# Batch 0's spectral stage: full-width forward matmuls on a three-part table, one product per pair of frequencies, and inverse tables loaded once and copied by Pool

## The chip, the cores and the metric

The kernel runs on one core of a Trainium2 chip. The core has a matrix engine (TensorE, PE in the profile, with its weight loads as PEld), a vector engine (VectorE, DVE), a scalar engine (ScalarE, ACT), a general engine (GpSimd, POOL) and a synchronisation engine (SyncE, SP) that here only issues transfers. Each engine works through its own queue in order and waits on semaphores. Sixteen DMA engines move data; a transfer is issued from Pool's queue (software descriptors; it may convert float32 to float16 and add on the way) or from SP's. The metric is the device time of one execution in microseconds; lower is better.

## The reference

For each of 8 batches, x (3008 x 256) is filtered along its 3008 positions in the frequency domain, and then a two-layer network with a PReLU is applied to every row:

```python
X = np.fft.rfft(x, axis=1)
F = (filt_r + 1j * filt_i)[None, :, :]
y = np.fft.irfft(X * F, n=x.shape[1], axis=1)
...
h = x @ w_in                                    # x is y as 24064 rows of 256; w_in 256 x 2048
g = np.maximum(h, 0.0) + alpha * np.minimum(h, 0.0)
return (g @ w_out).astype(np.float32)           # w_out 2048 x 256
```

Inputs and output are float32; the kernel computes in float16 with float32 sums in PSUM.

## The kernel before

**The transform.** 3008 = 47 x 64. A transform of 47 (piece_a), a twiddled transform of 64 for each of 24 frequencies k1 (piece_b), the product with the filter, the inverse of 64 (piece_c) and the inverse of 47 (piece_d) make the filter; between them the data is turned so that the next sum runs over partitions. The tables are constants in HBM: twf (forward) and twi (inverse), 128 partitions x 24 frequencies x 128 columns each, the left 64 columns and the right 64 holding the real and the imaginary outputs. filt_s holds the filter, filt_r on partitions 0 to 63 and filt_i on 64 to 127 at first. Frequencies are handled in twelve pairs kp, with k1 = 2 kp and 2 kp + 1.

**Batch 0 (class First)** comes alone at the start, with nothing else to do for the engines, and its turns are made on TensorE with an identity (turn_at, L273; piece_t, L310) instead of through DRAM. Its piece_b (L281) forms for a pair the real outputs twice (both halves of px) and the imaginary ones twice (both halves of pz), by eight matmuls with 64 table columns each (L288), into one PSUM tile of two banks (hps, two buffers). VectorE multiplies px and pz by the filter into uu and ww (L292, L293). piece_c (L296) multiplies uu with twi and ww with twx (L305, L306), where twx is twi with its partition halves exchanged and one negated; it adds up in PSUM (op, two buffers, psO) and ScalarE evicts it into v (L245). twx lies in the last three of the 17 buffers gtb, which the network needs later; its first quarter is formed by VectorE from twi (cross, L353), the rest is loaded.

**The order around it** is written out by hand. Pool issues, in this order: x of batch 0, four quarters of twf, filter and twi (the third load of each table takes two quarters) with twx, then w_in (win_s), w_out (wout_s), x of batch 1, and a copy of half of the filter to filts_s (L378). Each load from Pool waits until the eighth load before it has landed. SP issues five small constants and nothing else until batch 1's first save (L182). TensorE runs piece_a of batch 0 with some idle matmuls (warm), then in turn piece_c(kp), turn_at(kp + 3) and piece_b(kp + 2) (L372), then piece_t and piece_d, and then the network.

**The network and the other batches.** Rows go through in blocks of up to 512; a block takes 16 steps, each with two up matmuls (L421) of this block and the down matmuls (L440) of the block before. After every second step ScalarE evicts 1024 columns into gtb (L427) and VectorE applies the PReLU (L430, L431). A plan puts the transform's pieces of the later batches on numbered steps (put), where they are issued ahead of the step's matmuls. These batches use class Fft: piece_b multiplies px once with filt_s and once with filts_s (L200, L201), and a DMA adds one product's halves crosswise to the other (L203). For that filt_s must hold the real filter on both halves and filts_s the imaginary one, negated on one half: the four operations neg (L481) on steps 17, 20, 23 and 26 and a copy by DMA on step 29 (L485) see to it. Batch 1 starts with piece_a on steps 16 to 31, piece_b from step 40 on.

Of the kernel before, what the change touches and what calls it, by code (L numbers as in the profile page):

```python
# [10 lines left out]
FP16 = mybir.dt.float16  # L11
# [5 lines left out]
NK1 = 24  # L17
D = 256
# [18 lines left out]
def _build_consts():  # L37
# [27 lines left out]
    twf[:64, :, :64], twf[64:, :, :64] = c, s  # L65
    twf[:64, :, 64:], twf[64:, :, 64:] = -s * g, c * g
# [9 lines left out]
def kernel(  # L76
# [16 lines left out]
    twx_np = np.concatenate([twi_np[64:], -twi_np[:64]])  # L93
    twx_d = nc.inline_tensor(twx_np.astype(np.float16), name="c_twx")
# [21 lines left out]
    twf_s = konst.tile([128, NK1, 128], FP16, name="twf_s")  # L116
# [44 lines left out]
    class Fft:  # L161
# [31 lines left out]
        def piece_b(self, kp):  # L193
            px = bank().rearrange("p (k d) -> p k d", k=2)
            for kh in range(2):
                k1 = 2 * kp + kh
                nc.tensor.matmul(px[:, kh], twf_s[:, k1], self.at[:, k1], start=True, stop=True)  # L197
# [55 lines left out]
    class First(Fft):  # L253
# [27 lines left out]
        def piece_b(self, kp):  # L281
            hp = psH.tile([128, 2, 512], FP32, name="hps")
            px, pz = (hp[:, i].rearrange("p (k d) -> p k d", k=2) for i in range(2))
            for i, ps in enumerate((px, pz)):
                for kh in range(2):
                    k1 = 2 * kp + kh
                    for o in (0, 64):
                        nc.tensor.matmul(ps[o : o + 64, kh], twf_s[:, k1, 64 * i : 64 * i + 64],  # L288
                                         self.at[:, k1], start=True, stop=True)
            uu = p_uw.tile([128, 2, D], FP16, name="uu", bufs=4)  # L290
            ww = p_uw.tile([128, 2, D], FP16, name="ww")
            nc.vector.tensor_mul(uu, px, filt_s[:, 2 * kp : 2 * kp + 2])  # L292
            nc.vector.tensor_mul(ww, pz, filt_s[:, 2 * kp : 2 * kp + 2])  # L293
            self.uw[kp] = uu, ww
# [33 lines left out]
    for g in range(4):  # L328
        ka, kb = 6 * g, 6 * g + 6
        kc = slice(ka, 24 if g == 2 else kb)  # L330
        if g < 3:
            nc.gpsimd.dma_start(out=twf_s[:, kc], in_=twf_d.ap()[:, kc])
        load_filt(filt_s, 0, filt_r, ka, kb)
        load_filt(filt_s, 64, filt_i, ka, kb)
        if g < 3:
            nc.gpsimd.dma_start(out=twi_s[:, kc], in_=twi_d.ap()[:, kc])
        if g > 0:
            nc.gpsimd.dma_start(out=twx_s[:, ka:kb], in_=twx_d.ap()[:, ka:kb])
    for kt in range(2):
        nc.gpsimd.dma_start(out=win_s[:, kt], in_=moe_w_in[kt * 128 : (kt + 1) * 128])  # L340
    for q in range(2):
# [5 lines left out]

    def warm(n):
        pw = psO.tile([128, 2, D], FP32, name="op")
        for _ in range(n):  # L350
            nc.tensor.matmul(pw[:, 0, 0:128], id16, id16, start=True, stop=True)

    def cross(ka, kb):  # L353
        nc.vector.tensor_copy(twx_s[0:64, ka:kb], twi_s[64:128, ka:kb])
        nc.vector.tensor_scalar(twx_s[64:128, ka:kb], twi_s[0:64, ka:kb], -1.0, None, OP.mult)

    warm(36)
    for i in range(16):
        f0.piece_a(i, both[i % 2], i % 2 == 1)
        if i % 4 == 3:  # L360
            warm((16, 6, 5, 8)[i // 4])
    alp = psO.tile([128, 2, D], FP32, name="op")
    nc.tensor.transpose(alp[:, 0, 0:16], al16, id32)
    nc.vector.tensor_copy(al_s, alp[:, 0, 0:16])
    nc.vector.tensor_scalar(alm_s, al_s, 1.0, -1.0, OP.mult, OP.add)
    f0.turn_at(0, on_act)
    f0.turn_at(1, on_dve)
    f0.piece_b(0)
    cross(0, 6)
    f0.turn_at(2, on_act)  # L370
    f0.piece_b(1)
    for kp in range(12):  # L372
        f0.piece_c(kp, on_act)
        if kp < 9:
            f0.turn_at(kp + 3, on_act)
# [178 lines left out]
```

## Time and profile before

| | |
|---|---|
| time, median of 3 runs | 797.27 us (796.84 to 797.43) |
| the profiled execution, its own time | 795.65 us |
| its span, first to last instruction | 793.9 us |
| granted TensorE clock | 0.999 |
| busy over the span: PE, PEld | 775.0 us (98%), 538.5 us (68%) |
| DVE, ACT, POOL | 621.2 us (78%), 596.9 us (75%), 193.2 us (24%) |
| DMA moved | 100.58 MB, 127 GB/s on average |

The page is of one profiled execution. Busy time is when an engine had an instruction; the windows give it for stretches of the span, and the chain of waits goes back from one instruction to what released it, and so on. A row of the timeline gives start, duration, engine, line, operation, what is written and read with its shape (partitions x elements), and in brackets the idle time before it with its releaser. The landing of a transfer is when its last part has arrived.

### The profile page before, as it was taken

How to read it: one execution, taken by the hardware profiler on the slowest of the kernel's cores; microseconds unless marked ns; L12 is line 12 of the kernel's file. 1: busy time of each engine (PE TensorE's matmuls, PEld its weight loads, DVE VectorE, ACT ScalarE, POOL GpSimd, SP SyncE). 2: the span in 40 equal slices, each digit the busy share in tenths (PEclk: the TensorE clock that was granted, in tenths of full speed). 3: DMA queues.
4: the chain of work that ended last, by engine and by line, in shares of the span. 5: the costliest groups of instructions: out<-in, count | busy, mean ns of one | idle time of the engine just before them, and what ended most of it. 6: DMA issues, size and time to landing. Idle time of an engine off the chain costs nothing.

```text
span 793.9 us, 16103 instructions
## 1 busy us (share of the span) xinstructions
PE 775.0 (98%) x5956; PEld 538.5 (68%) x5956; DVE 621.2 (78%) x1377; ACT 596.9 (75%) x836; POOL 193.2 (24%) x269
## 2 busy tenths in 40 slices
PE   7999999999999999999999999999999999999997
PEld 6756656666677666766667666766667766766665
DVE  4797985788788787888787877887878888777773
ACT  3788678878778887788768887688867777787663
POOL 7510441153123221341223311242212222000000
PEclk9999999999999999999999999999999999999999
DMA  9967557695776648574684657656494333511111
GB/s 187 209 142 194 115 112 175 192 180 118 150 173 113 138 102 192 123 147 101 149 189 82 135 120 167 152 109 139 101 212 90 66 77 81 138 36 28 41 40 54
DMA packets 102310, 100.58 MB, mean 127 GB/s; under 512 B 11320, under 2 KB 92744, under 8 KB 102104
## 3 DMA queue, kind: packets, MB, share of 16 engines
q1 hardware_dynamic: 79512, 68.80, 32.9%
q0 software_dynamic: 22720, 30.75, 24.3%
q8 instruction: 47, 0.77, 0.4%
q14 instruction: 31, 0.25, 0.1%
HBM read 56.26 MB, written 46.66 MB: 130 GB/s over the span
## 4 chain that ended last, share of the span: by engine, by line
PE 89%; ACT 4%; DMA 3%; DVE 2%; issue 1%; SPq 0%; POOL 0%; ACTq 0%; DVEq 0%; POOLq 0%
PE hps L421 38%; PE op L440 38%; PE psF L177 3%; PE psF L238 3%; ACT gtb L427 2%; PE psF L216 2%; PE psF L197 2%; DMA uu<-ww 1%; DMA filt_s<-in_filt_i_dram 1%; DMA xs<-in_x_dram 1%; ACT asb L245 1%; PE hps L288 1%; PE psF L317 1%; DMA v_dram<-v 0%; DMA zt<-v_dram 0%
## 5 line engine op out<-in xcount | busy, mean ns | idle before, releaser
L427 ACT ACTIVATE gtb<-hps 128x1024 f16<-128x1024 f32 (+1 forms) x384 | 385.4, 1005 | 133.3 <-PE hps L421 127.9
L440 PE MATMUL op<-wout_s,gtb 128*128 128x256 f16 x3008 | 451.1, 272 | 0.6 <-DVE gtb L431 0.6
L421 PE MATMUL hps<-yT,win_s 128*128 128x512 f16 (+1 forms) x1536 | 449.2, 374 | 0.4 <-ACT gtb L427 0.2
L440 PEld LDWEIGHTS <-gtb 128*128 128x128 f16 x3008 | 293.2, 98 | 189.6 <-DVE gtb L431 0.9
L430 DVE TENSOR_SCALAR m<-gtb,alm_s 128x512 f16<-128x512 f16 (+1 forms) x768 | 235.7, 349 | 126.7 <-ACT gtb L427 124.4
L431 DVE TENSOR_TENSOR gtb<-gtb,m 128x1024 f16<-128x1024 f16 (+1 forms) x384 | 261.6, 681 | 19.9
L203 POOL DMA_DIRECT2D uu<-ww x168 | 140.6, 980 | 438.3 <-PE hps L421 322.1
L421 PEld LDWEIGHTS <-win_s 128*128 128x128 f16 x1536 | 145.3, 98 | 30.9 <-issue 3.1
L245 ACT ACTIVATE asb<-psF 96x512 f16<-96x512 f32 x112 | 66.2, 591 | 11.5 <-PE psF L177 11.4
L245 ACT ACTIVATE yT<-psF 128x376 f16<-128x376 f32 x120 | 57.1, 485 | 13.3 <-PE psF L238 12.8
L445 ACT ACTIVATE osb<-op 128x512 f32<-128x512 f32 x96 | 56.1, 585 | 6.1 <-issue 3.2
L245 ACT ACTIVATE v<-psF 128x512 f16<-128x512 f32 x84 | 49.4, 595 | 10.8 <-PE psF L216 10.0
L200 DVE TENSOR_TENSOR ww<-psF,filts_s 128x512 f16<-128x512 f32 x84 | 57.4, 684 | 0.0
L201 DVE TENSOR_TENSOR uu<-psF,filt_s 128x512 f16<-128x512 f32 x84 | 57.2, 681 | 0.0
L139 POOL DMA_DIRECT2D xs<-in_x_dram x64 | 43.9, 946 | 25.8 <-PE psF L177 15.0
L177 PE MATMUL psF<-xs,wf_s 94*96 94x512 f16 x112 | 42.7, 381 | 1.5 <-ACT v L245 1.0
L238 PE MATMUL psF<-wi_s,zt 96*128 96x94 f16 x504 | 40.3, 205 | 1.9 <-DMA zt<-v_dram 1.0
L238 PEld LDWEIGHTS <-zt 96*128 96x128 f16 x512 | 34.3, 97 | 6.2 <-issue 1.5
L216 PE MATMUL psF<-uu,twi_s 128*128 128x256 f16 x168 | 31.3, 273 | 2.3 <-ACT yT L245 0.9
L197 PE MATMUL psF<-at,twf_s 128*128 128x256 f16 x168 | 32.1, 273 | 0.3 <-ACT asb L245 0.2
L216 PEld LDWEIGHTS <-twi_s 128*128 128x128 f16 x168 | 15.7, 98 | 5.9 <-DMA uu<-ww 2.7
L197 PEld LDWEIGHTS <-twf_s 128*128 128x128 f16 x168 | 15.8, 98 | 2.8 <-DVE uu L201 0.7
(55 smaller groups left out, 173.3 us busy)
## 6 DMA issues: line engine op xcount, KB each, us to landing
out_dram<-osb SPq DMA_DIRECT2D x128, 128.0 KB
xs<-in_x_dram POOLq DMA_DIRECT2D x64, 188.0 KB, 5.4
a_dram<-asb SPq DMA_DIRECT2D x28, 384.0 KB
uu<-ww POOLq DMA_DIRECT2D x168, 64.0 KB, 2.9
v_dram<-v SPq DMA_DIRECT2D x112, 96.0 KB
zt<-v_dram SPq DMA_DIRECT2D x28, 384.0 KB
at<-a_dram SPq DMA_DIRECT2D x20, 384.0 KB
at<-a_dram SPq DMA_DIRECT2D x32, 96.0 KB
```

Of the source, the lines that this page charges most:

```text
L177: nc.tensor.matmul(ps[0:96], wf1_s, xs[:, o : o + 512], start=True, stop=True)
L197: nc.tensor.matmul(px[:, kh], twf_s[:, k1], self.at[:, k1], start=True, stop=True)
L200: nc.vector.tensor_mul(ww, px, filts_s[:, 2 * kp : 2 * kp + 2])
L203: nc.gpsimd.dma_start(out=uu[o : o + 64], in_=ww[64 - o : 128 - o], accum_op=OP.add)
L216: nc.tensor.matmul(pv[:, kh], twi_s[:, k1], u[:, kh], start=u is us[0], stop=u is us[-1])
L238: nc.tensor.matmul(ps[:, m], self.zt[:, 8 * g + 4 * mh + m, dh * 128 : dh * 128 + 128], wi3_s, start=True, stop=True)
L245: nc.scalar.activation(o, i, AF.Copy)
L421: nc.tensor.matmul(self.hps[:, j % 2, 0:tn], win_s[:, kt, j * 128 : (j + 1) * 128], yT[:, kt, self.t0 : self.t0 + tn], start=(kt == 0), st ...
L427: nc.scalar.activation(g[:, :, 0:tn], self.hps[:, :, 0:tn], AF.Copy)
L430: nc.vector.tensor_scalar(m[:, i, 0:tn], g[:, i, 0:tn], 0.0, a, OP.min, OP.mult)
L431: nc.vector.tensor_add(g[:, :, 0:tn], g[:, :, 0:tn], m[:, :, 0:tn])
L440: nc.tensor.matmul(self.op[:, si % 2], self.gts[k][:, 128 * si : 128 * si + 128], wout_s[:, k], start=(k == 0), stop=(k == 15))
```

## The change

- The forward table becomes three parts wide in SBUF: 64 columns with the imaginary outputs, 64 with the real ones, and a third part that is the first negated, formed on chip by third() from the loaded first part (ScalarE for frequencies 0 to 11, VectorE for 12 to 23). piece_b of batch 0 multiplies with columns 64 to 191 and with 0 to 127: four matmuls of 128 columns for a pair instead of eight of 64. The other batches use columns 64 to 191.
- VectorE multiplies both results of a pair by the filter in one operation, on 1024 columns of PSUM with the filter read twice, and writes into eight of the buffers gtb.
- twx is no longer a table of its own. SP loads partitions 0 to 63 of twi into the same partitions of twi_s, and 64 to 127 into those of twx_s (load_twi), in three parts, each after two one-element copies on VectorE or ScalarE that fix when it may start; Pool copies each half to the other partitions (both_halves). So in batch 0 both halves of each table are equal, and the signs stand in the forward table. Before the later batches a DMA copies partitions 64 to 127 of twx_s to twi_s, which then holds twi as before.
- The loads are re-ordered: twf still in quarters, the filter in parts of 4, 6, 7 and 7 frequencies, Pool's copies among them, w_in after six copies and w_out after all ten. The table twf is now loaded into the first 128 of 192 columns.
- The order of the pieces in batch 0: piece_b(kp + 2), turn_at(kp + 4), piece_c(kp - 2), with c7 to c11 in the last three turns, c10 evicted by VectorE.
- The filter for the later batches: filts_s is now two copies by DMA of the imaginary half, and neg writes the negated real half into filt_s, on steps 26, 29, 32 and 35. The copy on step 29 is gone.

```diff
--- before.py
+++ after.py
@@ -62,8 +62,8 @@
     ang = 2 * np.pi * s2[:, None, None] * kk[None, :, :] / NFFT
     c, s = np.cos(ang), np.sin(ang)
     twf = np.empty((128, NK1, 128))
-    twf[:64, :, :64], twf[64:, :, :64] = c, s
-    twf[:64, :, 64:], twf[64:, :, 64:] = -s * g, c * g
+    twf[:64, :, 64:], twf[64:, :, 64:] = c, s
+    twf[:64, :, :64], twf[64:, :, :64] = -s * g, c * g
     ec, es = c.transpose(2, 1, 0), s.transpose(2, 1, 0)
     gp = g[:, None, None]
     twi = np.empty((128, NK1, 128))
@@ -90,8 +90,6 @@
     wi3_d = nc.inline_tensor(wi3_np.astype(np.float16), name="c_wi3")
     twf_d = nc.inline_tensor(twf_np.astype(np.float16), name="c_twf")
     twi_d = nc.inline_tensor(twi_np.astype(np.float16), name="c_twi")
-    twx_np = np.concatenate([twi_np[64:], -twi_np[:64]])
-    twx_d = nc.inline_tensor(twx_np.astype(np.float16), name="c_twx")
     id_d = nc.inline_tensor(np.eye(128, dtype=np.float16), name="c_id")
     wfx_np = wf1_np.reshape(2 * N1, 2, 2, NK1).transpose(0, 3, 2, 1).reshape(2 * N1, 96)
     wfx_d = nc.inline_tensor(np.ascontiguousarray(wfx_np).astype(np.float16), name="c_wfx")
@@ -113,7 +111,7 @@
 
     wf1_s = konst.tile([2 * N1, 96], FP16, name="wf1_s")
     wi3_s = konst.tile([96, 2 * N1], FP16, name="wi3_s")
-    twf_s = konst.tile([128, NK1, 128], FP16, name="twf_s")
+    twf_s = konst.tile([128, NK1, 192], FP16, name="twf_s")
     twi_s = konst.tile([128, NK1, 128], FP16, name="twi_s")
     filt_s = konst.tile([128, NK1, D], FP16, name="filt_s")
     filts_s = konst.tile([128, NK1, D], FP16, name="filts_s")
@@ -194,7 +192,7 @@
             px = bank().rearrange("p (k d) -> p k d", k=2)
             for kh in range(2):
                 k1 = 2 * kp + kh
-                nc.tensor.matmul(px[:, kh], twf_s[:, k1], self.at[:, k1], start=True, stop=True)
+                nc.tensor.matmul(px[:, kh], twf_s[:, k1, 64:192], self.at[:, k1], start=True, stop=True)
             uu = p_uw.tile([128, 2, D], FP16, name="uu", bufs=4)
             ww = p_uw.tile([128, 2, D], FP16, name="ww")
             nc.vector.tensor_mul(ww, px, filts_s[:, 2 * kp : 2 * kp + 2])
@@ -280,18 +278,15 @@
 
         def piece_b(self, kp):
             hp = psH.tile([128, 2, 512], FP32, name="hps")
-            px, pz = (hp[:, i].rearrange("p (k d) -> p k d", k=2) for i in range(2))
-            for i, ps in enumerate((px, pz)):
+            for i in range(2):
                 for kh in range(2):
                     k1 = 2 * kp + kh
-                    for o in (0, 64):
-                        nc.tensor.matmul(ps[o : o + 64, kh], twf_s[:, k1, 64 * i : 64 * i + 64],
-                                         self.at[:, k1], start=True, stop=True)
-            uu = p_uw.tile([128, 2, D], FP16, name="uu", bufs=4)
-            ww = p_uw.tile([128, 2, D], FP16, name="ww")
-            nc.vector.tensor_mul(uu, px, filt_s[:, 2 * kp : 2 * kp + 2])
-            nc.vector.tensor_mul(ww, pz, filt_s[:, 2 * kp : 2 * kp + 2])
-            self.uw[kp] = uu, ww
+                    nc.tensor.matmul(hp[:, i, D * kh : D * kh + D], twf_s[:, k1, 64 - 64 * i : 192 - 64 * i],
+                                     self.at[:, k1], start=True, stop=True)
+            uw = gtb[:, 6 + kp % 8]
+            f = filt_s[:, 2 * kp : 2 * kp + 2].rearrange("p k d -> p (k d)").unsqueeze(1).to_broadcast([128, 2, 512])
+            nc.vector.tensor_mul(uw, hp, f)
+            self.uw[kp] = tuple(uw[:, i].rearrange("p (k d) -> p k d", k=2) for i in range(2))
 
         def piece_c(self, kp, evict):
             uu, ww = self.uw.pop(kp)
@@ -325,57 +320,93 @@
     nc.sync.dma_start(out=wf1_s, in_=wf1_d.ap())
     nc.sync.dma_start(out=wi3_s, in_=wi3_d.ap())
     make_identity(nc, id32)
-    for g in range(4):
-        ka, kb = 6 * g, 6 * g + 6
-        kc = slice(ka, 24 if g == 2 else kb)
-        if g < 3:
-            nc.gpsimd.dma_start(out=twf_s[:, kc], in_=twf_d.ap()[:, kc])
+
+    def third(eng, ka, kb):
+        o, i = twf_s[:, ka:kb, 128:192], twf_s[:, ka:kb, 0:64]
+        if eng is nc.scalar:
+            nc.scalar.activation(o, i, AF.Copy, scale=-1.0)
+        else:
+            nc.vector.tensor_scalar(o, i, -1.0, None, OP.mult)
+
+    def load_twf(ka, kb):
+        nc.gpsimd.dma_start(out=twf_s[:, ka:kb, 0:128], in_=twf_d.ap()[:, ka:kb])
+
+    def load_twi(ka, kb, ev):
+        ev(twi_s[0:1, ka, 0:1], id16[0:1, 0:1])
+        ev(twx_s[64:65, ka, 0:1], id16[64:65, 0:1])
+        nc.sync.dma_start(out=twi_s[0:64, ka:kb], in_=twi_d.ap()[0:64, ka:kb])
+        nc.sync.dma_start(out=twx_s[64:128, ka:kb], in_=twi_d.ap()[64:128, ka:kb])
+
+    def both_halves(ka, kb):
+        nc.gpsimd.tensor_copy(twi_s[64:128, ka:kb], twi_s[0:64, ka:kb])
+        nc.gpsimd.tensor_copy(twx_s[0:64, ka:kb], twx_s[64:128, ka:kb])
+
+    def load_g(ka, kb):
         load_filt(filt_s, 0, filt_r, ka, kb)
         load_filt(filt_s, 64, filt_i, ka, kb)
-        if g < 3:
-            nc.gpsimd.dma_start(out=twi_s[:, kc], in_=twi_d.ap()[:, kc])
-        if g > 0:
-            nc.gpsimd.dma_start(out=twx_s[:, ka:kb], in_=twx_d.ap()[:, ka:kb])
+
+    load_twf(0, 6)
+    load_g(0, 4)
+    load_twf(6, 12)
+    load_g(4, 10)
+    load_twf(12, 18)
+    load_g(10, 17)
+
+    def warm(n):
+        pw = psO.tile([128, 2, D], FP32, name="op")
+        for _ in range(n):
+            nc.tensor.matmul(pw[:, 0, 0:128], id16, id16, start=True, stop=True)
+
+    warm(36)
+    for i in range(16):
+        f0.piece_a(i, both[i % 2], i % 2 == 1)
+        if i % 4 == 3:
+            warm((16, 6, 5, 8)[i // 4])
+        if i == 7:
+            load_twi(0, 4, on_dve)
+        if i == 14:
+            load_twi(4, 12, on_act)
+    alp = psO.tile([128, 2, D], FP32, name="op")
+    nc.tensor.transpose(alp[:, 0, 0:16], al16, id32)
+    third(nc.scalar, 0, 6)
+    f0.turn_at(0, on_act)
+    f0.turn_at(1, on_dve)
+    nc.vector.tensor_copy(al_s, alp[:, 0, 0:16])
+    nc.vector.tensor_scalar(alm_s, al_s, 1.0, -1.0, OP.mult, OP.add)
+    f0.piece_b(0)
+    f0.turn_at(2, on_act)
+    f0.piece_b(1)
+    both_halves(0, 4)
+    load_twf(18, 24)
+    load_g(17, 24)
+    both_halves(4, 8)
+    both_halves(8, 12)
     for kt in range(2):
         nc.gpsimd.dma_start(out=win_s[:, kt], in_=moe_w_in[kt * 128 : (kt + 1) * 128])
+    third(nc.scalar, 6, 12)
+    f0.turn_at(3, on_act)
+    for kp in range(12):
+        if kp < 10:
+            if kp in (3, 6):
+                third(nc.vector, 2 * kp + 6, 2 * kp + 12)
+            f0.piece_b(kp + 2)
+        if kp < 8:
+            f0.turn_at(kp + 4, on_act)
+        if kp == 0:
+            load_twi(12, 24, on_act)
+            both_halves(12, 18)
+            both_halves(18, 24)
+        for k in {9: (7, 8), 10: (9, 10), 11: (11,)}.get(kp, (kp - 2,) if kp > 1 else ()):
+            f0.piece_c(k, on_dve if k == 10 else on_act)
     for q in range(2):
         nc.gpsimd.dma_start(
             out=wout_s[:, 8 * q : 8 * q + 8],
             in_=moe_w_out[1024 * q : 1024 * q + 1024].rearrange("(j p) d -> p j d", p=128))
     for c in range(4):
         xc[(1, c)] = load_x(1, c)
-
-    def warm(n):
-        pw = psO.tile([128, 2, D], FP32, name="op")
-        for _ in range(n):
-            nc.tensor.matmul(pw[:, 0, 0:128], id16, id16, start=True, stop=True)
-
-    def cross(ka, kb):
-        nc.vector.tensor_copy(twx_s[0:64, ka:kb], twi_s[64:128, ka:kb])
-        nc.vector.tensor_scalar(twx_s[64:128, ka:kb], twi_s[0:64, ka:kb], -1.0, None, OP.mult)
-
-    warm(36)
-    for i in range(16):
-        f0.piece_a(i, both[i % 2], i % 2 == 1)
-        if i % 4 == 3:
-            warm((16, 6, 5, 8)[i // 4])
-    alp = psO.tile([128, 2, D], FP32, name="op")
-    nc.tensor.transpose(alp[:, 0, 0:16], al16, id32)
-    nc.vector.tensor_copy(al_s, alp[:, 0, 0:16])
-    nc.vector.tensor_scalar(alm_s, al_s, 1.0, -1.0, OP.mult, OP.add)
-    f0.turn_at(0, on_act)
-    f0.turn_at(1, on_dve)
-    f0.piece_b(0)
-    cross(0, 6)
-    f0.turn_at(2, on_act)
-    f0.piece_b(1)
-    for kp in range(12):
-        f0.piece_c(kp, on_act)
-        if kp < 9:
-            f0.turn_at(kp + 3, on_act)
-        if kp < 10:
-            f0.piece_b(kp + 2)
-    nc.gpsimd.dma_start(out=filts_s[0:64], in_=filt_s[64:128])
+    nc.gpsimd.dma_start(out=twi_s[64:128], in_=twx_s[64:128])
+    for o in (0, 64):
+        nc.gpsimd.dma_start(out=filts_s[o : o + 64], in_=filt_s[64:128])
     warm(8)
     for i in range(4):
         f0.piece_t(i, both[i % 2], i % 2 == 1)
@@ -478,11 +509,10 @@
             put(d0 + gap * i, f0.piece_d, 4 * g + i, evs[i % len(evs)])
 
     def neg(ka, kb):
-        nc.vector.tensor_scalar(filts_s[64:128, ka:kb], filt_s[64:128, ka:kb], -1.0, None, OP.mult)
+        nc.vector.tensor_scalar(filt_s[64:128, ka:kb], filt_s[0:64, ka:kb], -1.0, None, OP.mult)
 
     for i in range(4):
-        put(17 + 3 * i, neg, 6 * i, 6 * i + 6)
-    put(29, lambda: nc.gpsimd.dma_start(out=filt_s[64:128], in_=filt_s[0:64]))
+        put(26 + 3 * i, neg, 6 * i, 6 * i + 6)
     plan_fft(1, 16, 1, 32, 40, 3, 0, 6, 92, 4, (20, 24, 74, 75))
     plan_fft(2, 66, 2, 97, 109, 4.5, 8, 12, 187, 4, (110, 114, 118, 122))
     for b in range(3, NB):
```

## The prediction

> **What bounds the kernel now.** I read the windows first, to see which stages have slack, then the chain of waits from 9 to 35 us, then the timeline of VectorE and Pool there, then the DMA view. Windows: length, busy time (and instructions) of PE, weight load, DVE, ACT, Pool, granted clock, DMA share, GB/s:
>
> ```profile
> 16.00:34.50 18.50, 16.55 (x234) 12.42 (x232) 16.08 (x26) 12.16 (x22) 12.49 (x23) 1.00 1.08 216
> 200.00:700.00 500.00, 499.44 (x3750) 347.57 (x3749) 402.62 (x903) 390.24 (x543) 120.85 (x156) 1.00 0.58 129
> ```
>
> From 200 us on TensorE is full and its work is unchanged, so only a shorter or longer opening can move the end. In 16 to 34.5 us, batch 0's spectral stage, VectorE, TensorE and the DMA engines are all nearly full. The chain (start, us, what):
>
> ```profile
> 9.87 6.34 DMA filt_s<-in_filt_i_dram
> ...
> 23.07 0.22 PE psF L278 x4
> 23.29 0.56 PE hps L288 x8
> 23.85 0.16 PE op L305
> ...
> 33.90 0.61 ACT v L245
> ```
>
> It starts with the landing of the filter's first part at 16.2; then a pair of frequencies (kp) passes every 1.37 us (uu starts at 16.34, and from 18.41 to 31.95 eleven of them), and the last eviction of v ends at 34.50. I call that the end of the stage. VectorE and Pool in it:
>
> ```profile
> 30.75 0.69 DVE L292 TENSOR_TENSOR uu<-hps,filt_s 128x512 f16<-128x512 f32 x1
> 31.36 0.68 DVE L293 TENSOR_TENSOR ww<-hps,filt_s 128x512 f16<-128x512 f32 x1
> 31.95 0.68 DVE L292 TENSOR_TENSOR uu<-hps,filt_s 128x512 f16<-128x512 f32 x1
> 17.66 0.35 DVE L354 COPY gtb<-twi_s 64x768 f16<-64x768 f16 x1
> 13.82 0.59 POOL L148 DMA_DIRECT2D filt_s<-in_filt_r_dram  x1 [0.37 <-DMA twf_s<-c_twf]
> 23.24 0.57 POOL L148 DMA_DIRECT2D filt_s<-in_filt_i_dram  x1
> 25.92 1.78 POOL L342 DMA_DIRECT2D wout_s<-in_moe_w_out_dram  x2
> ```
>
> A product of 512 columns lasts 0.68 us, but starts 0.60 after the one before: 1.21 a pair. Pool is an in-order queue, and a load waits for the landing of the eighth load before it. The first twf part landed by 13.8, the last filter load went out at 23.24 and lands about 4.2 later, at 27.4.
>
> **VectorE.** Twelve pairs of products become twelve of 1024 columns. Casts from PSUM cost 558 ns at 384 columns and about 690 at 512, 1.03 ns a column: 0.68+0.53=1.21 alone, 1.13 back to back. No such row is shown; bounds are 1.07 (512 columns saved of all fixed cost) and 1.38 (two rows of 0.69). I take 1.13, the nearest rows. The two cross() operations (0.35+0.36, on the chain at 17.66) go. Two third() operations of 384 columns come, 0.25 each: rows of 768 columns (0.355) and 1536 (0.557) give 0.26 ns a column on 0.15.
>
> **TensorE.** Eight 64-column matmuls (0.56) become four full ones; L440's four of the same 256 columns take 0.44. With the transposes (0.22) and the inverse (8 x 0.056=0.45) a pair needs 1.11 instead of 1.23, under VectorE's 1.13, so it sets no pace. But the inverse now runs four pairs behind, and c7 to c11 follow b11: after product 9 come b11 (0.55 with its signals), c7 (0.5), the evictions of c7, c8 and c9 on ScalarE (3 x 0.6; c11 has to wait for c9's, as the inverses share two PSUM buffers), c11 (0.5) and its own eviction (0.7): 4.05 in all. Today the end comes 1.27 after the last product (33.23 to 34.50).
>
> **ScalarE.** third(0,6) and third(6,12), bounded by 0.43 and 0.60 (evictions of 384 and 512 columns), taken as 0.47. The first stands ahead of the eviction of at(0); today ScalarE idles 0.76 before that, which covers it while twf lands by 14.3. The four one-element copies cost at most 0.2 each, in the same gap or beside VectorE's stage. If that cover fails, at(0), b0 and product 0 are late by as much.
>
> **The loads.** From 12.7 (last x) to 27.4 the queue moves four filter quarters and 1.97 MB of tables. In the fastest tenths of the window 12 to 16, where tables go, it shows about 360 GB/s, so tables take 5.5 us, the 24 filter frequencies 14.7-5.5-1.0 (lag of the slowest of 16 engines: 12.7+0.55+6x0.345=15.3 against 16.3 seen) = 8.2, 0.34 each. Now twi and twx move 0.79 instead of 1.18 MB before that last filter load; and twf's destination has pieces of 256 bytes, 768 to a quarter. Prices for a piece, by time x 16 engines over packets:
>
> ```profile
> q1 hardware_dynamic: 274, 0.06, 8.1%
> ...
> q0 software_dynamic: 1199, 0.69, 125.3%
> ```
>
> The first, 0 to 4 us, is mostly rows of 192 and 256 bytes: 19 ns. The second, 32 to 36 us, is wout, 1 KB read for 512 bytes written: 53 ns by elapsed time. A quarter costs 0.9 to 2.6 us instead of 0.55; I take 0.9, the rows of the same size. The schedule: first filter part (4 frequencies, behind 0.36 of twi) 12.7+0.36+0.9+1.4=15.35, lands 16.35. The next (6; twf 0.9, twi 0.73) ends 19.05, lands 20.05; the third (7) 22.4, lands 23.4; the last (twf 0.9, twi 1.09, 7 x 0.345) 26.8, lands 27.8.
>
> The Trainium skill ("DMA: Bandwidth & Descriptors", Specifications) asks for at least 512 bytes for line rate, below which the engine does read-modify-write. By this the quarter would stand near its slow end; the 19 ns row speaks against it, at light load only.
>
> **Pool's copies** are what no row shows: six of 64x512 (a each) and four of 64x768 (b), in order among the DMA issues. The last of the third filter group is issued by about 18.6 (as now). Then 2a, five issues 2.96 (filters 0.5 and 0.58 twice as today; twf 0.8, since 1024 pieces of wout take 0.89 and 192 of a filter 0.59), 4a, win 1.08, 4b. So both_halves are ready at 18.6+2a, 21.6+4a, 21.6+6a, 22.6+6a+2b, 22.6+6a+4b. PE asks for c2 at 24.0, for c9 near 31. Low bound: VectorE's copy, 0.355 for 768. High: the slowest copy rate shown, 558/384=1.45 ns an element, plus 0.1 fixed (a Pool MEMSET): a=0.84, b=1.21. A Pool twice as slow as that can't be excluded. I take 1.1 ns, between them: a=0.66, b=0.95, all ready by 30.4, just before c9. What waits in PE behind a late c is the next b, so VectorE too. Behind the copies stand win (issued 25.5 instead of 24.6, needed at 37.5, landing in 8 to 10 us), wout (30.4 instead of 25.9; 13 to land, needed at 49.0) and x of batch 1 (needed from 48.2): hidden at this price.
>
> The Trainium skill ("GPSIMD Engine Reference", Engine selection and Performance versus the Vector engine) calls one-input work on this engine roughly line rate, 1.03 to 1.8 cycles an element at 1.2 GHz. As an estimate that is 0.86 to 1.5 ns, the same span as my rows; by its first figure the copies bind nothing, by its second they cost a few tenths.
>
> **Costed at nothing.** twi_s restored and filts_s by two copies instead of one copy plus the filt_s copy at step 29: 1.2 MB more after x of batch 1, some 5 us, on engines that stand idle at 49 to 53 us; neg waits for it, at step 26 (about 64 us). Without that cover VectorE's queue, with m and gtb behind neg, would stop as long as the copy is late. neg is four operations of 0.557 as before, now ended before step 40. The six twi loads on SP's queue stand ahead of nothing until the a_dram save at 53.8.
>
> **Sum.** Product 0 at 16.4 (filter), product 1 ends 18.7, product 2 waits for the second filter part to 20.05; 2 to 4, third, 5 to 7, third: 20.05+6x1.13+0.5=27.35; product 8 waits to 27.8; product 9 ends 30.05, and 4.05 more is 34.1. Against 34.50: -0.4 us. The profiled execution took 795.65 (793.9 span and 1.75 around it), so 795.25; against the median of the runs, 797.27, it is **796.9**. Less work, but the filter's arrival takes the place of the pace.
>
> **Rivals.** (A) The loads are no limit: on 16 engines SP's twi overlaps the casts, pieces cost their bytes alone. Then 16.4+12x1.13+0.5=30.5 ends the products, and product 11 plus 1.8 (evictions) is 32.3: -2.2, 795.1. For it: DMA shares above 1, that is, packets overlap; against: loads are at 216 GB/s and more all through. (B) Slower, by Pool's copies: c9 waits for 22.6+6a+4b, then 1.95 to the end. It decides from 6a+4b=9.9, 1.45 ns an element; at 1.8 the end is 36.6 (+2.1, 799.4), at 2.2 it is 39.1 (+4.6, 801.9). For it: no Pool copy is shown, and Pool has ten in a stage where its queue is already busy 12.49 of 18.5 us; against: the rows' rates are below that. (C) 256-byte pieces cost 53 ns: four quarters 6.8 us later, +6.4, 803.7; at half of that +3. (D) The change doesn't do what it says: the wide product costs 1.38, so VectorE gains nothing: four products after 27.8, +0.6 in all, 797.9.
>
> **How the numbers follow.** 0.2% (1.6 us) is about what a measurement of this kernel can tell from no change. Forecast with (D): 0.44, all inside it. (A) 0.25, faster. (B) 0.23 and (C) 0.08, slower. The range goes from beyond (A), 794.6, to (B) at about 2 ns, 801.0; the forecast's own is 795.8 to 798.5.
>
> **What would show it.** Right: the wide product a row of near 1.2 us, waits of the third and ninth on filt_s, the end of v near 34. (A): no such wait, v near 32. (B): PE waiting on Pool ahead of the inverse. (C): third() and the forward matmuls waiting on twf_s. A stop of neg, or PE idle after 49 us that was not there, would make the whole argument wrong.

## The result and the profile after

| | before | after |
|---|---|---|
| median, first comparison | 796.77 us (795.49 to 799.30, 18 runs) | 795.10 us (793.90 to 796.85, 18 runs) |
| ratio, 95% interval | | 0.9977 [0.9969, 0.9985] |
| profiled execution, its own time | 795.65 us | 795.17 us |
| its span | 793.9 us | 793.4 us |

The change makes the kernel faster by 1.7 us, 0.21%, just past what a measurement of it can tell. Forecast were 796.9 us and "no change"; 795.10 lies below the forecast's own 795.8 to 798.5, inside the wide range. The two profiled executions, though, lie only 0.48 us apart. So there are two questions: what happened in the profile, and where the other microsecond came from.

The windows of the changed kernel (length, busy us and count of PE, weight load, DVE, ACT and Pool, granted clock, DMA share, GB/s):

```profile
16.00:34.50 18.50, 15.01 (x191) 12.68 (x189) 15.09 (x16) 12.38 (x24) 17.96 (x29) 1.00 1.07 194
200.00:700.00 500.00, 499.44 (x3751) 347.57 (x3750) 402.25 (x903) 390.26 (x543) 120.60 (x156) 1.00 0.58 129
```

TensorE does 1.5 us less in the spectral stage and VectorE 1.0 us less. Pool is busy for nearly all of it. From 200 us on the work is the same. VectorE's timeline there (start, duration, instruction, idle time before it and its releaser):

```profile
16.33 5.76 DVE L288 TENSOR_TENSOR gtb<-hps,filt_s 128x1024 f16<-128x1024 f32 x5 [0.21 <-PE hps L284]
22.01 0.25 DVE L329 TENSOR_SCALAR twf_s<-twf_s 128x384 f16<-128x384 f16 x1
22.62 3.53 DVE L288 TENSOR_TENSOR gtb<-hps,filt_s 128x1024 f16<-128x1024 f32 x3 [0.36 <-DMA filt_s<-in_filt_i_dram]
26.07 0.28 DVE L329 TENSOR_SCALAR twf_s<-twf_s 128x384 f16<-128x384 f16 x1
27.88 4.62 DVE L288 TENSOR_TENSOR gtb<-hps,filt_s 128x1024 f16<-128x1024 f32 x4 [1.53 <-PE op L301]
```

Five wide products take 5.76 us. One by itself takes 1.22 (in the chain below), so back to back one starts every (5.76-1.22)/4 = 1.14 us. Product 5 waits 0.36 us for the filter, and product 8 stands idle 1.53 us. The bracket names PE for that wait, but PE had long been done: the chain of waits of the same kernel (start, us, what) gives the transfer.

```profile
21.90 5.86 DMA filt_s<-in_filt_i_dram
27.88 0.06 DVE gtb L288
...
29.03 1.22 DVE gtb L288
30.30 0.61 PE hps L284 x4
...
32.71 0.60 ACT v L243
33.35 0.22 PE op L300
...
34.00 0.60 ACT v L243
```

The last filter part goes out at 21.90 and lands at 27.76. Four products follow, up to 32.50 (27.88+4.62), and then the inverses and evictions in turn; the end of the stage comes at 34.60, against 34.50 before. The stage has gained nothing: the wait has eaten the faster pace. Pool's copies in its timeline:

```profile
18.20 0.60 POOL L341 COPY twi_s<-twi_s 64x512 f16<-64x512 f16 x1
...
26.32 0.82 POOL L341 COPY twi_s<-twi_s 64x768 f16<-64x768 f16 x1
```

What this profiled execution won lies at the other end of the program. The last eviction of ScalarE, in the timelines of before and of after:

```profile
788.93 0.60 ACT L445 ACTIVATE osb<-op 128x512 f32<-128x512 f32 x1 [2.90 <-PE op L440]
```

```profile
788.83 0.60 ACT L476 ACTIVATE osb<-op 128x512 f32<-128x512 f32 x1 [2.90 <-PE op L471]
```

It ends 4.35 us ahead of the end of the span (793.88) before and 3.97 ahead (793.40) after. The last store lands 3.0 us after that eviction in both.

### The profile page after: what moved, and what is told of

It reads as the page before. It is cut to its first block, busy times and chain, and to the rows that moved or that the text cites. A ratio compares the mean times of both kernels' runs of the same rounds, so it can differ in the third digit from the quotient of the medians.

```text
span 793.4 us, 16044 instructions
## 1 busy us (share of the span) xinstructions
PE 773.1 (97%) x5908; PEld 538.5 (68%) x5908; DVE 619.8 (78%) x1368; ACT 597.9 (75%) x841; POOL 198.3 (25%) x275
## 4 chain that ended last, share of the span: by engine, by line
PE 88%; ACT 3%; DMA 3%; POOL 1%; DVE 1%; issue 1%; SPq 0%; ACTq 0%; POOLq 0%; DVEq 0%
PE hps L452 39%; PE op L471 39%; PE psF L175 3%; PE psF L236 3%; PE psF L214 2%; PE psF L195 2%; ACT gtb L458 2%; DMA twf_s<-c_twf 1%; DMA uu<-ww 1%; DMA filt_s<-in_filt_i_dram 1%; PE psF L312 1%; ACT asb L243 1%; POOL xs L137 1%; DMA zt<-v_dram 0%; DVE m L461 0%
## 5 line engine op out<-in xcount | busy, mean ns | idle before, releaser
L243 ACT ACTIVATE yT<-psF 128x376 f16<-128x376 f32 x120 | 57.1, 485 | 13.2 <-PE psF L236 12.7
L195 PE MATMUL psF<-at,twf_s 128*128 128x256 f16 x168 | 32.1, 272 | 0.3 <-ACT asb L243 0.2
```

Of the source, the lines that this page charges most:

```text
L195: nc.tensor.matmul(px[:, kh], twf_s[:, k1, 64:192], self.at[:, k1], start=True, stop=True)
L243: nc.scalar.activation(o, i, AF.Copy)
```

## The experiments

**The same two kernels again.** Single profiled executions differ, so each kernel has three profiles.

> The kernel before, unchanged, for a second look at its opening. Theory 'luck of the look': the profile shown of before caught an execution 1.1 us quicker than its median, so that its end of batch 0's last v eviction (34.50 us) is early; this look shows it later, 35 to 36.5, and the rest of the kernel as a rigid shift. Theory 'gain behind the opening': the end of v is again 34.5 within 0.2, and the time that the change saved lies after 48 us.

> The kernel before, a third look. Two looks showed the end of v at 34.50 and 34.48 us with spans of 793.9 and 794.3, while its median run is near 797.2, some 1.2 above these two. Theory 'opening': in the usual run the opening itself ends later, at 35 to 36. Theory 'middle': the opening is a machine pace (VectorE and TensorE) and ends at 34.5 again, and the extra time of a usual run lies between 78 and 145 us, where batch 1 waits for transfers (0.5 us between the two looks already).

> The changed kernel, unchanged. Its profile had the end of v at 34.60, with product 8 waiting until 27.88 for the last filter part (27.8 forecast). Theory 'luck of the look': the end of v moves between looks with the landing of the slowest DMA engine, 33 to 35; the time is 0.9977 of before within 0.001. Theory 'gain behind the opening': end of v 34.6 within 0.2 again.

> The changed kernel once more, as the partner of the next run on one chip. From its two earlier medians (795.10 and 795.32): 794.9 to 795.5 us, ratio to before 0.997 to 0.998. In its profile the end of batch 0's v lies between 33.3 and 34.6 us, with the wait of one product on the last filter part deciding where, and from the last eviction of the program to its end 3.97 us.

| profile | time | end of the stage | product 8 starts |
|---|---|---|---|
| before, three profiles | 795.65, 796.19, 795.93 us | 34.50, 34.48, 34.7 us | |
| after | 795.17 us | 34.60 us | 27.88 us |
| after_again | 794.46 us | 33.35 us | 26.62 us |
| after_third | 794.83 us | 34.25 us | 27.55 us |

Medians: after_again 795.32 us (12 runs), 0.997 [0.9956, 0.9984] of before; after_third 794.98 us (11 runs), 0.9973 [0.9963, 0.9983]. VectorE's last four products in after_again:

```profile
26.62 4.62 DVE L288 TENSOR_TENSOR gtb<-hps,filt_s 128x1024 f16<-128x1024 f32 x4 [0.17 <-DMA filt_s<-in_filt_i_dram]
```

The same transfer landed 1.3 us sooner (26.50) and the stage ended 1.25 sooner: what follows the last filter part is the same in these two, and its landing sets the end. The profiles of before end the stage within 0.24 us of each other, and all three are quicker than its usual run, so they don't show where a usual run loses its time. In after_third the last filter part landed about as soon as in after_again, at 26.62, but product 8 started only at 27.55. VectorE's and Pool's timelines show why:

```profile
26.78 0.85 DVE L329 TENSOR_SCALAR twf_s<-twf_s 128x384 f16<-128x384 f16 x1
27.55 2.34 DVE L288 TENSOR_TENSOR gtb<-hps,filt_s 128x1024 f16<-128x1024 f32 x2
```

```profile
26.69 0.82 POOL L342 COPY gtb<-gtb 64x768 f16<-64x768 f16 x1
```

third(), 0.25 us at its shortest, took 0.85: it began 0.09 us after a copy of Pool and ended 0.12 us after it (27.63 against 27.51). Its other instance in this profile began 0.09 us after a copy of 0.61 (22.74) and took 0.64. The products, which read PSUM, kept their pace beside the same copies.

**The wide product undone.**

```diff
-            nc.vector.tensor_mul(uw, hp, f)
+            for i in range(2):
+                nc.vector.tensor_mul(uw[:, i], hp[:, i], f[:, i])
```

> The changed kernel with the wide product undone: two products of 512 columns a pair, back to back 1.21 us instead of 1.13 to 1.15, all else as changed. Theory 'filter' (the landings of the filter set the opening, products 2, 5 and 8 wait for them): the waits shrink, the end of v moves by at most 4 x 0.07 = 0.3 us, time within 0.4 us of the changed kernel. Theory 'VectorE' (its pace sets it): 12 x 0.07 = 0.8 us later or more.

Measured: 796.25 us (795.16 to 797.48, 12 runs), 0.9987 [0.9975, 1.0]; +0.9 us against after_again on the same chip. In its profile the last eight products waited as after's four did:

```profile
27.92 4.87 DVE L289 TENSOR_TENSOR gtb<-hps,filt_s 128x512 f16<-128x512 f32 x8 [0.43 <-DMA filt_s<-in_filt_i_dram]
```

4.87 against 4.62: behind the last filter part the wide product is worth 0.25 us, and the stage ended at 34.78. The profile speaks for the theory 'filter', but the median went past that theory's 0.4 us, to the 0.8 or more of 'VectorE'. The rest of the 0.9 us the profile doesn't show. Low clock isn't it: the five runs at 0.999 and 1.000 have a median of 795.92, 0.8 above those of the changed kernel (795.09, in the table further down). Where the part lands at 26.5, as in after_again, all twelve pairs count, 12 x 0.06 to 0.08 = 0.7 to 1.0 us; that this is how a usual run goes is argued, not shown.

**The full-width matmuls undone.**

```diff
-                    nc.tensor.matmul(hp[:, i, D * kh : D * kh + D], twf_s[:, k1, 64 - 64 * i : 192 - 64 * i],
-                                     self.at[:, k1], start=True, stop=True)
+                    for o in (0, 64):
+                        c = 64 - 64 * i + o
+                        nc.tensor.matmul(hp[o : o + 64, i, D * kh : D * kh + D], twf_s[:, k1, c : c + 64],
+                                         self.at[:, k1], start=True, stop=True)
```

> The changed kernel with piece_b's four full-width matmuls of a pair undone to eight of 64 columns. Theory that the last filter part sets the opening: TensorE needs some 0.12 us more a pair, 1.23 against 1.15 of the wide product, and only the last four products come after that part, so +0.3 us at most: 795.1 to 795.6 us. Rival, that the full-width matmuls carry the gain: twelve pairs of 0.12 us, +1.4 us, 796.6 us, about the kernel before.

Measured: 795.32 us (794.52 to 796.54, 11 runs), 0.9982 [0.9973, 0.9991]; +0.3 us against after_third. That is the filter's theory, in the median. Its windows and products hold something else:

```profile
14.00:18.00 4.00, 3.74 (x39) 2.88 (x37) 2.43 (x6) 2.21 (x7) 3.79 (x8) 0.57 0.99 191
18.00:23.00 5.00, 4.59 (x64) 3.00 (x61) 5.00 (x5) 3.80 (x9) 4.85 (x9) 1.00 1.13 219
```

```profile
17.56 5.75 DVE L290 TENSOR_TENSOR gtb<-hps,filt_s 128x1024 f16<-128x1024 f32 x5 [0.23 <-PE hps L286]
...
27.85 4.62 DVE L290 TENSOR_TENSOR gtb<-hps,filt_s 128x1024 f16<-128x1024 f32 x4 [0.35 <-DMA filt_s<-in_filt_i_dram]
```

TensorE's granted clock was 0.57 from 14 to 18 us (column before the last two), and product 0 came at 17.56 instead of 16.33. Yet product 8 started as in after: the wait for the filter took up the whole 1.23 us.

**Pool's copies undone: SP loads both halves.**

```diff
     nc.sync.dma_start(out=twi_s[0:64, ka:kb], in_=twi_d.ap()[0:64, ka:kb])
+    nc.sync.dma_start(out=twi_s[64:128, ka:kb], in_=twi_d.ap()[0:64, ka:kb])
...
-    nc.gpsimd.tensor_copy(twi_s[64:128, ka:kb], twi_s[0:64, ka:kb])
-    nc.gpsimd.tensor_copy(twx_s[0:64, ka:kb], twx_s[64:128, ka:kb])
+    pass
```

The second half of twx is loaded likewise, and one-element copies fix the start of the new loads too.

> The changed kernel without Pool's ten copies: SP loads each half of the inverse tables twice, 0.79 MB more ahead of the last filter part, while Pool issues the last table part and filter part 1.2 us earlier, and w_out and x earlier by up to 7 us. Theory 'filter': 0.79 MB at some 360 GB/s are 2.2 us; the last filter part lands up to 2.2 us later, less what the earlier issue gives back; time 0.5 to 2 us longer than the changed kernel. Theory 'Pool' (its copies hold the loads and the inverse back): time 0.5 to 1 us shorter.

Measured: 798.34 us (797.23 to 800.41, 12 runs), 1.0013 [1.0, 1.0026]; +3.0 us against after_again, past the 0.5 to 2 us that were expected. VectorE:

```profile
31.19 3.58 DVE L288 TENSOR_TENSOR gtb<-hps,filt_s 128x1024 f16<-128x1024 f32 x3 [3.58 <-DMA filt_s<-in_filt_i_dram]
```

The last filter part, issued 0.6 us earlier than in after, landed at 31.07: 3.3 us later than in after and 4.6 later than in after_again. The tables' 0.79 MB more, on the same sixteen engines, are the cause by theory 'filter', though by its 360 GB/s they take only 2.2; the rest isn't explained, and w_out and x of batch 1, which now go out up to 5.6 us earlier, weren't held apart. Half clock from 32.1 to 35.5 us adds to this profile. In all the copies keep the filter early, and without them the rest of the change brings no gain.

**The inverse issued ahead.** c6 to c8 go before the last forward pairs, and ScalarE evicts all:

```diff
+        for k in {8: (6, 7), 9: (8,)}.get(kp, (kp - 2,) if 1 < kp < 8 else ()):
+            f0.piece_c(k, on_act)
...
-        for k in {9: (7, 8), 10: (9, 10), 11: (11,)}.get(kp, (kp - 2,) if kp > 1 else ()):
-            f0.piece_c(k, on_dve if k == 10 else on_act)
+        if kp > 8:
+            f0.piece_c(kp, on_act)
```

> The changed kernel with the inverse matmuls of pair kp-2 issued ahead of the forward ones of kp+2, c6 to c8 before the last two forward pairs, c9 to c11 as their products end, all evicted by ScalarE. In the changed kernel c6 to c11 stood behind the product that waits for the last filter part, and the end of v came 2.1 us after the last product (32.50 to 34.60, and 31.24 to 33.34). Theory 'filter, then the tail': end of v 1.2 to 1.4 after the last product, so 0.7 to 0.9 us less than the changed kernel. Rival 'Pool': c2 asked for Pool's copies at 23.4 and got them at 23.9; asked earlier it holds the forward matmuls back and the gain is gone or turned into a loss of up to 0.5 us.

> The order of c_ahead again, beside the changed kernel on the same chip. Theory that what follows the last product counts in full: its tail after the last product is 1.3 us instead of 2.1, so its median is 0.6 to 1.0 us below that of after_third. Rival, that the earlier 0.8 us was the difference between two chips: medians within 0.3 us of each other.

Measured: 794.42 us (12 runs), 0.9968 [0.9957, 0.9978]; again 794.76 us (8 runs), 0.997 [0.996, 0.9981], 0.2 us under after_third on the same chip. The tail is 1.3 us instead of 2.1 in both profiles, but the opening ahead of it was late. In c_ahead_again:

```profile
20.29 3.49 DVE L288 TENSOR_TENSOR gtb<-hps,filt_s 128x1024 f16<-128x1024 f32 x3 [1.10 <-PE psF L276]
...
28.46 4.71 DVE L288 TENSOR_TENSOR gtb<-hps,filt_s 128x1024 f16<-128x1024 f32 x4
```

Product 8 started without a wait for the filter, but 0.6 to 1.8 us later than in the profiles of after; third() took 0.66 and 0.86 us here beside Pool's copies. The 1.10 us ahead of product 2 are put down to PE, but the second filter part landed at 20.11 (18.43 to 19.25 in the profiles of after), 0.18 before that product. In c_ahead product 8 did wait for the last part, which landed at 28.37. So a landing made the opening late in both; whether the new order delays the landings wasn't tried. The 0.6 to 1.0 us expected side by side didn't come. It is at least as quick as the changed kernel and has the lowest medians of the study; whether it is quicker stays open.

**The last inverse table four pairs later.** c_ahead, with the last load of twi and its copies at pair 4:

```diff
-        if kp == 0:
+        if kp == 4:
```

> As the kernel with the inverse ahead, and SP's last load of the inverse tables (0.39 MB) started by ScalarE four pairs later, some 5 us, so that it stands behind the last forward table part and shares the engines with the last filter part at most. In the changed kernel it was issued at 19.2 and the last table part landed 2.3 us after the part ahead of it (22.5 to 25.0) instead of about 1. Theory 'filter': the last filter part lands up to 1.1 us earlier (26.5 to 25.5 or 27.8 to 26.7), and the end of v is 0.5 to 1.1 us earlier than with the inverse ahead alone. Rival 'Pool': Pool's copies for pairs 6 to 11 start when this load lands, at 27 instead of 26.3, w_out and x behind them, c6 waits, and nothing is gained.

Measured: 802.43 us (801.20 to 804.16, 6 runs), 1.0072 [1.0054, 1.0089]; +8.0 against c_ahead. Pool and then VectorE:

```profile
32.41 0.82 POOL L341 COPY twi_s<-twi_s 64x768 f16<-64x768 f16 x1 [6.55 <-DMA twi_s<-c_twi]
```

```profile
27.04 2.34 DVE L288 TENSOR_TENSOR gtb<-hps,filt_s 128x1024 f16<-128x1024 f32 x2
37.41 1.23 DVE L288 TENSOR_TENSOR gtb<-hps,filt_s 128x1024 f16<-128x1024 f32 x1 [8.04 <-PE hps L284]
```

SP issued the load at 25.45, behind w_in, which Pool had issued at 24.73, and its first half landed some 7 us later. An inverse that waits for its table holds the forward matmuls queued behind it on PE, and VectorE stops 8 us, part of it at half clock (32.9 to 39.7 us). What a late inverse does in rival (B) is seen here, but from a late load and not from slow copies, which took 0.82 us as ever; in the changed kernel its only trace is 0.5 us of PE at L301 for Pool's copy, under VectorE's work.

**The end of the program.** Six loads of 192 bytes from SP are added to the kernel before, at the start and, in the second kernel, on steps 640 to 650:

```diff
+    pad = konst.tile([6, 96], FP16, name="pad")
+    for i in range(6):
+        nc.sync.dma_start(out=pad[i : i + 1], in_=wf1_d.ap()[i : i + 1])
```

> The kernel before with six more transfers of 192 bytes from SP at the start, which no one uses; the changed kernel also issues six more from SP. From the last eviction to the end both looks of before took 4.35 us and three of the changed kind 3.97 (4.12 with twelve more), while the last store landed 3.0 after that eviction in all. Theory 'order of the last waits' (the program's end waits for SP's eight DMA semaphores one after the other, and the number of transfers decides which of them is last): the end takes 3.97 here too, and the time is 0.4 us shorter than before. Theory 'chance or other cause': 4.35 and no change.

> The kernel before with six loads of 192 bytes from SP in the middle of the last batch (steps 640 to 650), where SP is idle, instead of at the start. Theory that the end of the program depends on which of SP's eight DMA semaphores the last store has: the opening is that of the kernel before, from the last eviction to the end 3.97 instead of 4.35 us, median 0.4 us below before (ratio 0.9995). Rival, that the shorter end belongs to the changed opening: 4.35 us and no difference. If the six loads cost anything by themselves, as the same six at the start seemed to (+1.4 us), a small step shows near 640 us of the span.

Measured: 798.54 us (12 runs), 1.0022 [1.0005, 1.0038], and 797.74 us (12 runs), 1.0012 [1.0, 1.0024]. The end shrank from 4.35 to 3.98 and 4.01 us, as expected: the last instructions wait for SP's eight DMA semaphores one after another, some 0.06 us each. The last store's is the first of the eight in that order before, and the seventh with six more transfers; the changed kernel issues six twi loads. In tables_by_dma, with twelve more, it is the fifth, and the end took 4.12. But the 0.4 us didn't show in the time: both kernels came out slower. The profiles show two reasons. One: between 285 and 640 us piece_b waited up to 0.5 us for its rows from DRAM, three times, and PE was busy 0.9 us less there in before_six_more and 1.1 us less in before_six_late; the kernel before has no such wait. In before_six_late:

```profile
PE psF L197 <- DMA at<-a_dram: 0.3, 1, 0.3
```

Its cause wasn't tried (the six transfers move the order of the semaphores, the tile moves others by 192 bytes). Two, in the windows of before_six_late and then of before:

```profile
14.00:18.00 4.00, 3.74 (x34) 2.98 (x33) 2.16 (x6) 1.12 (x3) 4.00 (x8) 0.50 1.07 215
18.00:23.00 5.00, 4.61 (x40) 3.15 (x38) 3.82 (x8) 1.68 (x3) 3.55 (x8) 0.50 1.07 249
```

```profile
14.00:18.00 4.00, 2.72 (x32) 1.86 (x31) 2.96 (x7) 1.23 (x3) 3.46 (x7) 1.00 1.08 231
18.00:23.00 5.00, 4.57 (x69) 3.63 (x69) 4.69 (x9) 3.26 (x6) 4.25 (x9) 1.00 1.02 250
```

Up to step 640 these two do the same work. But here the clock stood at 0.50 from 14 to 23 us, PE started 40 matmuls in the second window instead of 69, and the eight matmuls of a pair took 0.99 us instead of 0.56. The stage ended 2.84 us later, at 37.34. That is nearly all of this run's lost clock: 9 to 10 us at half speed are some 5 of 798 us, and its mean clock was 0.994. before_six_more had such a stretch from 18.4 to 21.8 us (+1.39). In the usual run of these two low clock isn't the reason: at 0.999 and 1.000 their medians are 798.2 (6 runs) and 797.7 (9), against 796.65 before. The first reason covers that only in part, and the rest stays open.

**All runs by their mean granted clock.** Low clock is no matter of the added loads: the runs list it for every execution. Medians in us, with the number of runs, over all comparisons that list the clock:

| mean clock | before | after | narrow_matmuls | c_ahead, both |
|---|---|---|---|---|
| 0.999 and 1.000 | 796.65 (44) | 795.09 (26) | 794.93 (4) | 794.50 (12) |
| 0.997 and 0.998 | 797.64 (29) | 794.91 (11) | 795.14 (3) | 794.36 (2) |
| 0.996 and less | 799.53 (11) | 795.54 (4) | 796.32 (4) | 794.62 (6) |
| all | 797.05 (84) | 795.17 (41) | 795.32 (11) | 794.54 (20) |

The kernel before loses 2.9 us from the first row to the third, the changed one 0.45, and with narrow matmuls 1.4. The third row isn't like for like: seven of before's eleven runs lie at 0.992 and 0.993, and none of the changed kernel's is under 0.994. A straight line through all runs is fairer: 0.44 us for each 0.001 of clock before, 0.11 after, 0.33 with narrow matmuls (standard errors 0.05, 0.07 and 0.10). The share of runs under 0.999 is somewhat lower after (15 of 41) than before (40 of 84). So the clock drops for both, and the kernel before pays more for it. The reason is argued, not shown: its TensorE needs 1.23 us for a pair that takes 1.37, and at half speed there is no room; after the change TensorE has less to do, and behind it stands a wait for the filter that takes up a late start. The groups were made after the runs; no kernel was run to force the clock, and the small ones are weak. Where the run without a profile loses its clock isn't listed. Profiles show it in the first 25 us in four cases (two_products, narrow_matmuls and the two with six loads) and later in two (tables_by_dma and c_ahead_late_twi, where PE had stood waiting).

## Why the prediction was right or wrong

**The opening was right at full clock.** The stage was to end at 34.1, 0.4 us sooner. Three profiles gave 34.60, 33.35 and 34.25, on average 34.07; those of before average 34.56: -0.5. The mechanism is the one forecast, the last filter part in the place of the pace, in two of the three; in the third third() was later still. That the size agrees so well is in part luck, as the terms show.

**Its terms.** The wide product, forecast at 1.13 back to back and 1.21 alone, measured 1.14 and 1.22. The filter's parts, forecast at 16.35, 20.05, 23.4 and 27.8, landed at 14.69, 18.43, 22.49 and 27.76 in the first profile: the start was put 1.7 us late, after the one landing of before (16.22) that its profile held (15.65 and 15.79 in the other two), and the later parts took longer than forecast by as much in all. So product 0 waited for PE and product 2 for nothing, and that 27.8 came out is luck: two errors cancel. In the other two profiles the last part landed at 26.50 and 26.62, and product 2 did wait, for a part that landed at 18.72 and 19.25; a landing differs from profile to profile by over a microsecond, which one profile couldn't show. From product 9's end to the end of the stage 4.4 us passed instead of 4.05. third() at 0.25 us was too low beside Pool's copies: up to 0.86, ahead of product 8 where it matters. The rows of before couldn't show that, as VectorE's two copies there met only DMA issues on Pool. What was costed at nothing behind the stage cost nothing: from 49 to 78 us PE is busy 28.28 us in the first profile of both kernels.

**Pool's copies** took 0.60 and 0.82 us, forecast 0.66 and 0.95; the last was ready at 29.78, forecast 30.4. Rival (B) needed 1.45 ns an element and the rows have (0.82-0.60)/256 = 0.86. The Trainium skill ("GPSIMD Engine Reference", Performance versus the Vector engine) has 1.03 cycles an element at the low end, at 1.2 GHz; 0.86 ns are 1.03 such cycles, so the trace agrees with that end.

**256-byte pieces.** The second quarter of twf, behind which no twi stood, landed 1.20, 0.76 and 0.86 us after the part ahead of it in the three profiles; 0.9 was forecast, and 2.6 was rival (C). The prediction's 0.55 us for a quarter before was an estimate. In the three profiles of before the second quarter landed 0.68, 1.17 and 0.58 us after the load ahead of it, so that the short pieces cost anything isn't shown. The Trainium skill ("DMA: Bandwidth & Descriptors", Specifications) has less than line rate below 512 bytes; these landings are too scattered to show it, and they rule out the slow row's price.

**What failed is the last step of the sum**: "against the median of the runs, 797.27, it is 796.9". It carried a gain read from one execution over to the median, as if both kernels stood equally far above their profiles. Its median of three runs was also 0.5 us above that of the first comparison (796.77). The profiles of before average 795.92, those of after 794.82: -1.1, of which -0.5 is the opening, -0.37 the end of the program and -0.2 waits between 80 and 145 us that differ from profile to profile. The medians, 797.05 and 795.17, are -1.9 apart. The other 0.8 us is that before's usual run lies 1.1 us above its profiles and after's only 0.35 above. Low clock is the smaller share of that: among the runs at 0.999 and 1.000 before still lies 0.7 above its profiles and after 0.3, so 0.45 of the 0.8 us is left at full clock, and this stays open. Two prices of nothing were wrong with it: the full-width matmuls ("sets no pace") seem to pay at low clock (narrow_matmuls lies 0.8 above the changed kernel there, with four runs each), and the end of the program, left out of the account, pays 0.37 us in every profile.

**The rivals.** The time is that of (A), 795.1, but its mechanism is not: product 8 waited for the filter, the stage never ended before 33.35, and (A) had 32.3. (B) did not act here: the copies were quicker than it needs, and c_ahead_late_twi shows only what a late inverse would do. (C) needed the slow row's price, which the landings don't show. (D) fell with the 1.14 us.

## What to carry to other kernels

A profile is one execution: before a gain read from it is set against a median, look at how far the runs lie from their profiles and at what clock, and price an edit at the low clock too. Work taken off an engine that sets no pace at full clock may be what keeps the stage whole at half; here that is likely, not shown. Where a landing sets a stage, replace bytes ahead of it by a copy on an engine with room, but look at what runs beside that copy.

## What was unexpected of the hardware

- TensorE's granted clock fell to 0.50 in the opening of some executions and not of others; of two kernels that do the same work up to there (before and before_six_late) one had it and one not. From windows of 1 us the stretches last 3.4 us in narrow_matmuls (from 14.2), two_products (from 12.7), before_six_more (from 18.4) and tables_by_dma (from 32.1), 6.8, twice as much, in c_ahead_late_twi (from 32.9), and 10.2, three times as much, in before_six_late (from 12.8). The windows of before_six_more around its stretch:

```profile
17.00:18.00 1.00, 0.20 (x3) 0.15 (x2) 0.95 (x3) 0.11 (x1) 1.00 (x3) 1.00 1.25 237
18.00:19.00 1.00, 0.66 (x7) 0.66 (x7) 0.97 (x3) 0.00 (x0) 1.00 (x3) 0.69 0.84 276
19.00:20.00 1.00, 1.00 (x11) 0.75 (x10) 0.60 (x2) 0.73 (x2) 1.00 (x3) 0.50 1.00 312
...
21.00:22.00 1.00, 1.00 (x12) 0.86 (x12) 0.98 (x2) 0.34 (x1) 0.27 (x1) 0.60 1.19 184
22.00:23.00 1.00, 1.00 (x17) 0.80 (x18) 0.41 (x1) 0.74 (x2) 0.84 (x2) 1.00 1.15 270
```

  The Trainium skill ("TensorE: Matmul & The Clock Gate", What's actually happening) has a gate that halves the clock after an idle window of some 3.4 us, the windows running free of the program. The trace agrees in the 0.50, the lengths and the changing start. On idleness the record says something too: in the 3.41 us ahead of the drop PE was busy 0.00 us in c_ahead_late_twi and 0.25 in tables_by_dma, but 1.68 to 1.94 us in the four openings. Such a window is no idle one, and before was busy 1.73 us from 9.40 to 12.81, where before_six_late with 1.68 fell, and kept its clock; that only the place of the free-running windows differs would fit, but no run here was made to show it.
- A copy of VectorE that starts during one of Pool's ends 0.1 us after it (third(), 0.25 us by itself, became 0.64, 0.66, 0.85 and 0.86). The Trainium skill ("SBUF — State Buffer", Who interferes with whom) has a pair of ports that the two engines share as an exclusive lock in some of VectorE's modes. The trace agrees. In the profile of c_ahead a Pool copy that began together with third(), at 28.01, took 0.94 instead of 0.82: there the loser was Pool.
- The end of the program depends on the number of SP's transfers: 4.35, 4.12 or 3.97 to 4.01 us after the last eviction as its semaphore is the first, the fifth or the seventh of eight to be waited for, while the last store lands 3.0 us after that eviction each time.
